# Float32r splits for the second attention products of batches 0 and 1, and for ten of sixteen first-block output products

## Chip, core and metric

The kernel runs on one core of one Trainium2 chip. The metric is the device time of one execution in microseconds, taken as the median of several runs. Engines are named as the profile names them: PE is TensorE (PEld its weight loads), DVE VectorE, ACT ScalarE, POOL GpSimd, SP SyncE, which here issues nearly all transfers.

## What is computed

The reference, cut to its core:

```python
def _attn_ref(q, k, v):            # batch 8, heads 8, seq 576, head_dim 64
    k_p = k.reshape(B, H, Sp, 8, D).mean(axis=3)      # 72 pooled rows
    v_p = v.reshape(B, H, Sp, 8, D).mean(axis=3)
    scores = scale * np.matmul(q, k_p.transpose(0, 1, 3, 2))
    attn = softmax(scores)          # exp, sum + 1e-9
    return np.matmul(attn, v_p)

x = attention output as 4608 tokens x 512
h = x @ w_in;  x = (h * cos(h)) @ w_out               # 512 -> 2048 -> 512
g = x @ w_gate; x = (silu(g) * (x @ w_val)) @ w_out2  # 512 -> 1536 -> 512
```

## The kernel before

**Stages.** The program is a start-up (attention of batch 0, conversion of the weights), then the first MLP, into which attention of batches 1 to 7 is woven, then the second MLP. The first MLP goes over 9 blocks of 512 tokens (n), each in 16 *slots* of 128 hidden columns (f). A slot (n, f) is: `pe_h` (lines 537 to 539), 12 products of 128x512 into the PSUM tile `h`; `turns` (547, 548) and `cosine` (569 to 573), which make `w` = h·cos h on ACT and DVE; `parts` (584 to 587), which splits `w` into `gh` + `gl`; and two slots later `pe_y`, which adds the slot's share of the output to the four PSUM tiles `acc`.

**Two ways of a product.** float32 data go through TensorE either as float32, one instruction that the trace shows as two MATMUL records, or as float32r, where each operand is split into a high part (an ACT cast) and a low part (a DVE subtraction) and three products are issued: high·high, high·low, low·high. `pe_y` uses float32 for `n == 0 and f < Y32` (line 599), the split else (606 to 608). `Y32` is 16 before, so all of block 0 is float32: no `parts`, no `wo_high` in it.

**Second attention product.** `do_pt` transposes the normalised probabilities `pm` of a tile of 128 (or 64) tokens into PSUM (`pt`, 64 of the 72 pooled rows of each head, and `px`, the remaining 8 rows of all heads) and copies them to `pth` and `ptx`. `prep_v` makes the stationary operands from the pooled v. `do_av` then multiplies, per pair of heads p (4 of them) and group of tokens (256 + 256 + 64 in batch 0, 256 + 320 in the others), into `av`, and ACT writes the result into `ring` (399). For batches below `ACTB` = 2, `do_av` issues two float32 products, `vmh`·`pth` and `vl1`·`ptx`; for the others five float32r products (`vmh`·`pth`, `vmh`·`ptl`, `vml`·`pth`, `vl1`·`ptx`, `vl2`·`ptx`). Batch 0's tokens, split into `xhl` (514 to 516), are the first block's input, so the first `pe_h` waits for groups 0 and 1 of batch 0.

**Order.** The first step of the program is a string of letters: `s` scores, `x` softmax, `p` transposes, `a` av products, `v` prep_v, `V0`/`K`/`U` pooled sums on DVE, `f`/`F`/`G` pieces of weight conversion (`fill`), `i`/`o` loads of weights, `X` the split into `xhl`:

```python
    "s0 s1 f4 x0 s2 p0 V0 v x1 p1 f6 s3 s4 F3 a0 x2 p2 x3 p3 a1 w i1 q G2 K0 K1 K2 U0 X i11 o2 "
    "x4 b f6 "
```

A tile scheduler then reorders the instructions on each engine by its own estimates, so that the code's order is only its input. The weights arrive as 64-bit floats in `st_i` (w_in) and `st_o` (w_out); four integer operations on ACT and DVE (477, 482, 487, 494) turn a piece of 128x512 into float32 (`ce_i`, `wo`), and for w_in lines 1010 (ACT) and 994 (DVE) split it into `wa`. The raw float32 w_out stays in `wo_raw`, from which float32 `pe_y` reads directly and `wo_high` (553) and line 586 make the split one. Batch 1's slots are 1 to 14, batch 2 begins at 17. `do_norm` (338 to 350) makes `pm`; tile 1's `pm` lies in `vst` and tiles 2 and 3's in `kst`, the buffers of raw v and k.

Of the kernel before, what the change touches and what calls it, by code (L numbers as in the profile page):

```python
# [8 lines left out]
F32 = mybir.dt.float32  # L9
F32R = mybir.dt.float32r  # L10
# [15 lines left out]
def fused_kernel(  # L26
# [18 lines left out]
    nc = tc.nc  # L45
    B, H, S, D = q.shape
# [58 lines left out]
    kT = p1a.tile([P, NP, 2 * SP], F32, name="kT")  # L105
    av_tiles = {}

    def av_tile(nm, b):

        kind = F32 if b < ACTB else F32R  # L110
        if (nm, kind) not in av_tiles:
            shape = {"v": [P, NP, P], "p": [P, NP, PTW], "x": [P, PTW]}["x" if nm == "ptx" else nm[0]]
            t = av_tiles[nm, kind] = p1a.tile(shape, kind, name=f"{nm}_{b}", tag=nm)
            if nm in ("vmh", "vml", "vl2"):
                nc.gpsimd.memset(t if kind is F32 else t.bitcast(F32), 0.0)
        return av_tiles[nm, kind]

    nc.gpsimd.memset(kT, 0.0)
    for nm in ("vmh", "vml", "vl1", "vl2", "pth", "ptl", "ptx"):
        av_tile(nm, 0)  # L120

    def raw_tile(nm):
        return chain.tile([P, 2, TB], F32, name=nm, tag="raw", bufs=2)
# [125 lines left out]
            nc.scalar.mul(to[:, :, SM:], ps[rows, 2 * P :].rearrange("d (s p) -> d p s", p=NP), -EXP_SCALE)  # L249

    def prep_v(b):
        vmh, vml, vl1, vl2 = (av_tile(nm, b) for nm in ("vmh", "vml", "vl1", "vl2"))
        vp = vps.pop(b)
        if b < ACTB:
            for r in range(2):
                rows, cols = slice(r * SM, (r + 1) * SM), slice(r * D, (r + 1) * D)
                nc.scalar.mul(vmh[rows, :, cols], vp[rows, :NP], 1.0 / POOL)
            nc.vector.tensor_mul(
                vl1[:SM].rearrange("q p (r d) -> q r p d", r=2),
                vp[:SM, NP : NP + 1].rearrange("q (a o) d -> q a o d", a=1).to_broadcast([SM, 2, NP, D]),  # L260
                mask[:SM].rearrange("q (p r o) -> q r p o", r=2, o=1).to_broadcast([SM, 2, NP, D]),
            )
            return
        for r in range(2):
            rows, cols = slice(r * SM, (r + 1) * SM), slice(r * D, (r + 1) * D)
            nc.scalar.mul(vmh[rows, :, cols], vp[rows, :NP], 1.0 / POOL)
            nc.vector.scalar_tensor_tensor(
                out=vml[rows, :, cols], in0=vp[rows, :NP], scalar=1.0 / POOL, in1=vmh[rows, :, cols],
                op0=ALU.mult, op1=ALU.subtract,
            )  # L270
        t = p1a.tile([P, H, SP], F32, name=f"vt_{b}", tag="e")[:, :, :D]
        nc.vector.tensor_mul(
            t, vp[:, NP : NP + 1].to_broadcast([P, H, D]), mask.rearrange("p (h o) -> p h o", o=1).to_broadcast([P, H, D])
        )
        t = t.rearrange("q (p r) d -> q r p d", r=2)
        h2 = vl1.rearrange("q p (r d) -> q r p d", r=2)
        l2 = vl2.rearrange("q p (r d) -> q r p d", r=2)
        for r in range(2):
            nc.scalar.copy(h2[:, r], t[:, r])
            nc.vector.tensor_sub(l2[:SM, r], t[:SM, r], h2[:SM, r])  # L280
# [49 lines left out]
    def do_norm(b, t, pm=None):  # L330
        n = TILES[t][1]
        e = es.pop((b, t))[:n]
        if b < ACTB:
            sm = sms.pop((b, t))[:n]
        else:
            sm = p1a.tile([P, H, 1], F32, name=f"sm_{b}_{t}", tag="sm", bufs=2)[:n]
            nc.vector.reduce_sum(sm[:, :, 0], e, axis=AX.X)
        nc.vector.tensor_scalar_add(sm, sm, 1e-9)
        nc.vector.reciprocal(sm, sm)
        if pm is None:  # L340
            pm = p1a.tile([P, H * SM + P], F32, name=f"pm_{b}_{t}", tag="pm")
        pms[b, t] = pm
        nc.vector.tensor_mul(
            pm[:n, : H * SM].rearrange("q (h s) -> q h s", h=H), e[:, :, :SM], sm.to_broadcast([n, H, SM])
        )

        for g in range(2):
            left = pm[:n, H * SM + g * SM : H * SM + (g + 1) * SM].rearrange("q (h s) -> q h s", h=H)
            if g == 0:
                nc.vector.tensor_mul(left, e[:, :, SM:], sm.to_broadcast([n, H, SL]))  # L350
            elif b >= ACTB:
                nc.vector.tensor_copy(pm[:n, H * SM + SM :], pm[:n, H * SM : H * SM + SM])

# [930 lines left out]
```

## Time and profile before

| | us |
|---|---|
| median of 3 runs | 1787.25 |
| runs from, to | 1786.49, 1788.84 |
| profiled execution, its own time | 1786.07 |
| its span | 1784.3 |
| PE busy in the span | 1737.2 (97%) |
| DVE busy | 1169.0 (66%) |
| ACT busy | 996.1 (56%) |

The profiled execution takes 1.8 us more than its span. In the rows below a timeline line is: start, length, engine, source line, operation, what it writes and reads, shape, count of records run together; in square brackets the idle time of the engine ahead of it and what ended that. Matmul records overlap, so the time of a product is the distance between starts. PEclk is the granted TensorE clock, 1.00 for 2.4 GHz.

### The profile page before, as it was taken

Reading aid. Unit: us, or ns where it says so; the run is one execution under the profiler, and the core shown is the slowest. Engines: PE = TensorE matmul, PEld = TensorE weight load, DVE = VectorE, ACT = ScalarE, POOL = GpSimd, SP = SyncE. Lnnn points to the kernel's source line nnn. Section 1 sums busy time; section 2 is a strip of 40 time slices with the busy share of each in tenths; the row PEclk is TensorE's granted clock in tenths of the full one; section 3 lists DMA queues with packets and bytes.
Section 4 is the critical chain, followed back from the end, with each engine's and each line's share of the span. In section 5 each row is a group of like instructions: output and inputs, shape, how many; then the busy total and the mean of one; then the engine's idle time right before and its main releaser. Section 6 shows DMA issues by size and latency. Waiting matters only on the chain.

```text
span 1784.3 us, 23241 instructions
## 1 busy us (share of the span) xinstructions
PE 1737.2 (97%) x8076; PEld 1444.5 (81%) x8076; DVE 1169.0 (66%) x2006; ACT 996.1 (56%) x1815; POOL 122.1 (7%) x217
## 2 busy tenths in 40 slices
PE   4979999999999999999999999999999999999998
PEld 3546588888888888888888778888888888999998
DVE  6695377867767677687675677853684377458346
ACT  5576477767667767677575565433443344344333
POOL 0131300403003011000000000000000000000000
PEclk9989999999999999999999999999999999999999
DMA  9553244646576455575775587675567657777772
GB/s 232 162 162 105 82 149 145 194 133 205 131 228 208 118 201 145 188 213 160 230 265 182 192 321 270 202 274 195 195 208 257 197 191 225 298 255 244 298 253 90
DMA packets 240244, 357.00 MB, mean 200 GB/s; under 512 B 141696, under 2 KB 147840, under 8 KB 240128
## 3 DMA queue, kind: packets, MB, share of 16 engines
q1 hardware_dynamic: 235440, 354.35, 61.5%
q10 hardware_dynamic: 4688, 1.18, 0.3%
q8 instruction: 64, 1.05, 0.2%
q14 instruction: 52, 0.43, 0.1%
HBM read 285.74 MB, written 69.73 MB: 199 GB/s over the span
## 4 chain that ended last, share of the span: by engine, by line
PE 89%; DMA 4%; DVE 4%; ACT 2%; issue 1%; POOL 0%; SPq 0%; ACTq 0%; DVEq 0%; POOLq 0%
PE X L791 14%; PE oX L921 8%; PE h L537 7%; PE h L538 7%; PE h L539 7%; PE acc L606 7%; PE Y L791 7%; PE acc L608 7%; PE acc L607 7%; PE oY L921 4%; PE av L393 3%; PE Z L791 3%; PE acc L599 2%; PE oZ L921 2%; PE s L308 2%; DMA w2r<-w_dram 1%
## 5 line engine op out<-in xcount | busy, mean ns | idle before, releaser
L791 PE MATMUL X<-t_P,wc 128*128 128x512 f32 (+1 forms) x1080 | 232.9, 368 | 2.3 <-ACT u L840 2.3
L537 PE MATMUL h<-xhl,wa 128*128 128x512 f32 x576 | 232.0, 403 | 1.3 <-DVE w L573 1.3
L539 PE MATMUL h<-xhl,wa 128*128 128x512 f32 x576 | 225.9, 392 | 0.0
L538 PE MATMUL h<-xhl,wa 128*128 128x512 f32 x576 | 225.9, 392 | 0.0
L791 PEld LDWEIGHTS X<-t_P,wc 128*128 128x128 f32 x1080 | 196.5, 188 | 29.1 <-ACT u L840 4.0
L606 PE MATMUL acc<-gh,wo_ring 128*128 128x512 f32 x448 | 179.3, 400 | 0.0
L607 PE MATMUL acc<-gl,wo_ring 128*128 128x512 f32 x448 | 174.8, 390 | 0.0
L608 PE MATMUL acc<-gh,wo_ring 128*128 128x512 f32 x448 | 174.8, 390 | 0.0
L547 ACT ACTIVATE w<-h,few 128x512 f32<-128x512 f32 x144 | 98.9, 687 | 121.3 <-PE h L539 121.0
L548 DVE SCALAR_TENSOR_TENSOR w<-w,h 128x512 f32<-128x512 f32 x144 | 98.2, 682 | 68.8 <-ACT w L547 68.5
L537 PEld LDWEIGHTS h<-xhl,wa 128*128 128x128 f32 x576 | 109.1, 189 | 27.8 <-issue 3.8
L573 DVE SCALAR_TENSOR_TENSOR w<-w,h 128x512 f32<-128x512 f32 x144 | 98.4, 683 | 49.9 <-ACT w L570 48.2
L538 PEld LDWEIGHTS h<-xhl,wa 128*128 128x128 f32 x576 | 108.9, 189 | 23.7 <-issue 2.4
L539 PEld LDWEIGHTS h<-xhl,wa 128*128 128x128 f32 x576 | 108.9, 189 | 23.0
L587 DVE TENSOR_TENSOR gl<-w,gh 128x512 fp32r<-128x512 f32 x128 | 90.9, 710 | 51.0 <-ACT gh L584 50.1
L584 ACT CAST gh<-w 128x512 fp32r<-128x512 f32 x128 | 78.9, 616 | 69.3 <-DVE w L573 47.3
L569 ACT ACTIVATE w<-w 128x512 f32<-128x512 f32 x144 | 91.1, 633 | 46.1 <-DVE w L548 45.1
L843 DVE TENSOR_TENSOR p<-p,X 128x512 f32<-128x512 f32 (+1 forms) x60 | 37.8, 632 | 116.8 <-PE X L791 108.6
L126 ACT CAST xhl<-pst 128x1024 fp32r<-128x1024 f32 (+1 forms) x70 | 67.7, 968 | 71.3 <-PE oX L921 26.1
L921 PE MATMUL oX<-xhl,wc 128*128 128x512 f32 (+1 forms) x480 | 102.7, 368 | 0.0
L608 PEld LDWEIGHTS acc<-gh,wo_ring 128*128 128x128 f32 x448 | 84.1, 188 | 18.6
L606 PEld LDWEIGHTS acc<-gh,wo_ring 128*128 128x128 f32 x448 | 84.2, 188 | 17.0 <-issue 0.8
(196 smaller groups left out, 3377.2 us busy)
## 6 DMA issues: line engine op xcount, KB each, us to landing
wc<-wc_dram SPq DMA_DIRECT2D x273, 512.0 KB
wo_ring<-wo_dram SPq DMA_DIRECT2D x112, 512.0 KB
wc_dram<-wc SPq DMA_DIRECT2D x42, 512.0 KB
wc_dram<-ow SPq DMA_DIRECT2D x42, 256.0 KB
y_dram<-yo SPq DMA_DIRECT2D x18, 512.0 KB
w_dram<-ce_w SPq DMA_DIRECT2D x36, 256.0 KB
st_i<-in_moe_w_in_dram SPq DMA_DIRECT2D x16, 512.0 KB
st_o<-in_moe_w_out_dram SPq DMA_DIRECT2D x16, 512.0 KB
```

The costliest lines, as they stand in the source:

```text
L537: nc.tensor.matmul(ps, whi, xhl[0][:, 0, c], start=c == 0, stop=False)
L538: nc.tensor.matmul(ps, whi, xhl[0][:, 1, c], start=False, stop=False)
L539: nc.tensor.matmul(ps, wlo, xhl[0][:, 0, c], start=False, stop=c == KC - 1)
L547: nc.scalar.activation(w, h, AF.Identity, bias=magic)
L548: nc.vector.scalar_tensor_tensor(out=w, in0=w, scalar=MAGIC, in1=h, op0=ALU.subtract, op1=ALU.subtract)
L569: nc.scalar.activation(w, w, AF.Sin, scale=PI)
L573: nc.vector.scalar_tensor_tensor(out=w, in0=w, scalar=1.0, in1=h, op0=ALU.subtract, op1=ALU.mult, reverse0=True)
L606: nc.tensor.matmul(acc[n][i], a[:, cols], xh, start=f == 0, stop=False)
L607: nc.tensor.matmul(acc[n][i], a[:, cols], xl, start=False, stop=False)
L608: nc.tensor.matmul(acc[n][i], b[:, cols], xh, start=False, stop=f == NF1 - 1)
L791: nc.tensor.matmul(ps[:, :hb], w, t[:, x, c, :hb], start=first and c == 0 and n == 0, stop=c == 1 and n == 2, skip_group_check=not first,)
L921: nc.tensor.matmul(banks[key][m][:, :hb], u, x[:, b, i, :hb], start=first_ and j == i == k == 0, stop=j == NJ - 1 and i == 1 and k == 2, s ...
```

## The change

`Y32` goes from 16 to 6: in block 0, slots 6 to 15 get `parts` (two ACT casts and two DVE subtractions a slot) and 12 float32r products in `pe_y` in place of 4 float32 ones. The branches `b < ACTB` go out of `prep_v`, `do_norm`, `do_pt`, `do_av` and `av_tile`: batches 0 and 1 get `vml`, `vl2`, `ptl`, full `ptx`, and five float32r products in place of two float32 ones. The tiles for these are made once, in float32r, and no longer again at batch 2. Lines after are 11 to 20 lower than before (537 becomes 517, 599 becomes 579).

```diff
-    Y32 = NF1
+    Y32 = 6
...
     def prep_v(b):
...
-        if b < ACTB:
-            for r in range(2):
-                rows, cols = slice(r * SM, (r + 1) * SM), slice(r * D, (r + 1) * D)
-                nc.scalar.mul(vmh[rows, :, cols], vp[rows, :NP], 1.0 / POOL)
-            nc.vector.tensor_mul(
-                vl1[:SM].rearrange("q p (r d) -> q r p d", r=2),
...
-            return
...
-            elif b >= ACTB:
+            else:
                 nc.vector.tensor_copy(pm[:n, H * SM + SM :], pm[:n, H * SM : H * SM + SM])
...
     def do_pt(b, t):
...
-        if b < ACTB:
-            nc.scalar.copy(pth[:, :, o : o + n], ps)
-            px = psum.tile([SM, n], F32, name=f"px_{b}_{t}", tag="att", bufs=2)
-            nc.tensor.transpose(px, pm[:n, NP * P : NP * P + SM], ident[:n, :n])
-            nc.scalar.copy(ptx[:SM, o : o + n], px)
-            return
         nc.scalar.copy(pth[:, :, o : o + n], ps)
         nc.vector.tensor_sub(ptl[:, :, o : o + n], ps, pth[:, :, o : o + n])
...
-        if b < ACTB:
-            terms = [(vmh, pth[:, p, o : o + n])]
-            terms += [(vl1[:SM], ptx[:SM, o : o + n])]
```

The scheduler moves instructions with this. On DVE in the start-up, from the sign step of `ce_i_3` to the normalisation of tile 1 (`vst`), the kernel before has these; `vl` is the operand for the last 8 pooled rows, `sm_1` tile 1's sums:

```order
L494 SCALAR_TENSOR_TENSOR ce_i_3_185<-st_i_3_131,ce_i_3_185 128x512
L258 TENSOR_TENSOR vl_0_97<-vp_309,few 64x2x4x64
L338 TENSOR_SCALAR sm_1_240<-sm_1_240 128x8
L487 SCALAR_TENSOR_TENSOR ce_i_0_193<-st_i_0_161,ce_i_0_193 128x512
L339 RECIPROCAL sm_1_240<-sm_1_240 128x8
L994 TENSOR_TENSOR wa_3_265<-ce_i_3_185,wa_3_265 128x512
L343 TENSOR_TENSOR vst<-vst,sm_1_240 128x512
L350 TENSOR_TENSOR vst<-vst,sm_1_240 128x64
```

After, from the first subtraction of tile 0's transposes:

```order
L352 TENSOR_TENSOR ptl<-pt_0_301,pth 128x4x128
L356 TENSOR_TENSOR ptx<-px_0_308,ptx 64x128
L256 SCALAR_TENSOR_TENSOR vml<-vp_312,vmh 64x4x64
L261 TENSOR_TENSOR vt_320<-vp_312,few 128x8x64
L974 TENSOR_TENSOR wa_3_265<-ce_i_3_185,wa_3_265 128x512
L256 SCALAR_TENSOR_TENSOR vml<-vp_312,vmh 64x4x64
L269 TENSOR_TENSOR vl_98<-vt_320,vl_97 64x4x64 x2
L327 TENSOR_SCALAR sm_1_240<-sm_1_240 128x8
L467 SCALAR_TENSOR_TENSOR ce_i_0_193<-st_i_0_161,ce_i_0_193 128x512
L328 RECIPROCAL sm_1_240<-sm_1_240 128x8
L474 SCALAR_TENSOR_TENSOR ce_i_0_193<-st_i_0_161,ce_i_0_193 128x512
L332 TENSOR_TENSOR vst<-vst,sm_1_240 128x512
```

Two subtractions on tile 0 and five more for v now stand between `ce_i_3` and tile 1's `vst`; the mask product for `vl` (258) is gone.

On PE where the first output product of block 0 stands (slot 0, `w_0`; `s_1` are batch 1's scores of tile 1, `qp` transposes of q), before:

```order
L539 MATMUL h_3_727<-xhl,wa_3_265 128x512
L308 MATMUL s_1_0_754<-kT,qT_1_656 128x144 x2
L308 MATMUL s_1_1_764<-kT,qT_1_656 128x144 x2
L599 MATMUL acc_0_696<-w_0_563,wo_449 128x512
L599 MATMUL acc_1_697<-w_0_563,wo_449 128x512
L599 MATMUL acc_2_698<-w_0_563,wo_449 128x512
L599 MATMUL acc_3_699<-w_0_563,wo_449 128x512
L293 MATMUL qp_2_774<-ident,q_453 128x128 x4
L599 MATMUL acc_0_696<-w_1_628,wo_449 128x512
```

After:

```order
L519 MATMUL h_2_727<-xhl,wa_3_265 128x512
L282 MATMUL qp_1_715<-ident,q_496 128x128 x4
L297 MATMUL s_1_0_820<-kT,qT_1_714 128x144 x2
L297 MATMUL s_1_1_830<-kT,qT_1_714 128x144 x2
L579 MATMUL acc_0_754<-w_0_607,wo_492 128x512
L579 MATMUL acc_1_755<-w_0_607,wo_492 128x512
L579 MATMUL acc_2_756<-w_0_607,wo_492 128x512
L579 MATMUL acc_3_757<-w_0_607,wo_492 128x512
L517 MATMUL h_3_793<-xhl,wa_0_139 128x512
L518 MATMUL h_3_793<-xhl,wa_0_139 128x512
```

The first output product now stands behind `h_2` and ahead of `h_3`; before it stood behind `h_3`, with slot 1's output next.

On PE, slot 6's output product (`s_3` are scores of batch 1's tile 3), before:

```order
L308 MATMUL s_3_1_1072<-kT,qT_3_902 128x144 x2
L599 MATMUL acc_0_696<-w_6_945,wo_449 128x512
L599 MATMUL acc_1_697<-w_6_945,wo_449 128x512
L599 MATMUL acc_2_698<-w_6_945,wo_449 128x512
L599 MATMUL acc_3_699<-w_6_945,wo_449 128x512
L293 MATMUL qp_4_1082<-ident,q_453 128x64 x4
```

After:

```order
L586 MATMUL acc_0_754<-gh_6_1074,wo_6_1076 128x512
L587 MATMUL acc_0_754<-gl_6_1075,wo_6_1076 128x512
L588 MATMUL acc_0_754<-gh_6_1074,wo_6_1076 128x512
L586 MATMUL acc_1_755<-gh_6_1074,wo_6_1076 128x512
L587 MATMUL acc_1_755<-gl_6_1075,wo_6_1076 128x512
L588 MATMUL acc_1_755<-gh_6_1074,wo_6_1076 128x512
L586 MATMUL acc_2_756<-gh_6_1074,wo_6_1076 128x512
L587 MATMUL acc_2_756<-gl_6_1075,wo_6_1076 128x512
L588 MATMUL acc_2_756<-gh_6_1074,wo_6_1076 128x512
L586 MATMUL acc_3_757<-gh_6_1074,wo_6_1076 128x512
L587 MATMUL acc_3_757<-gl_6_1075,wo_6_1076 128x512
L588 MATMUL acc_3_757<-gh_6_1074,wo_6_1076 128x512
```

Four float32 products on `w_6` became twelve on `gh_6` and `gl_6`.

## Rows read from the trace of the kernel before

**Rows 1.** Windows: us, busy by engine with counts, granted clock, DMA share, GB/s.

```profile
80.00:100.00 20.00, 11.58 (x54) 8.69 (x54) 19.31 (x36) 19.61 (x56) 7.22 (x9) 0.90 0.10 29
...
120.00:140.00 20.00, 15.71 (x54) 9.87 (x52) 16.34 (x28) 14.15 (x35) 7.76 (x11) 0.91 0.62 193
...
180.00:200.00 20.00, 20.00 (x65) 10.74 (x64) 4.06 (x6) 6.13 (x15) 8.47 (x17) 1.00 0.20 57
...
80.00:124.00 44.00, 33.85 (x126) 21.34 (x125) 42.23 (x74) 34.46 (x83) 18.09 (x24) 0.92 0.38 121
```

**Rows 2.** Timeline of PE, start-up to slot 6's output product (columns above).

```profile
46.55 1.19 PE L393 MATMUL av<-pth,vmh 128*128 128x256 f32 x2 [0.79 <-issue]
...
55.73 1.11 PE L361 MATMUL pt<-ident,kst 128*128 128x128 f32 x4
...
59.36 1.22 PE L393 MATMUL av<-pth,vmh 128*128 128x256 f32 x2 [0.52 <-ACT pth L363]
...
68.56 0.79 PE L537 MATMUL h<-xhl,wa 128*128 128x512 f32 x1
...
70.44 0.63 PE L538 MATMUL h<-xhl,wa 128*128 128x512 f32 x1
70.86 0.63 PE L539 MATMUL h<-xhl,wa 128*128 128x512 f32 x1
...
97.92 6.11 PE L599 MATMUL acc<-w,wo 128*128 128x512 f32 x8 [7.12 <-DVE wo L494]
...
126.55 1.03 PE L293 MATMUL qp<-ident,q 128*128 128x128 f32 x4 [4.29 <-ACT e L318]
...
149.85 2.74 PE L599 MATMUL acc<-w,wo 128*128 128x512 f32 x6
```

**Rows 3.** Timeline of PE, slot 15's float32 output, then block 1's first split one.

```profile
215.57 3.59 PE L599 MATMUL acc<-w,wo 128*128 128x512 f32 x8
219.00 1.14 PE L308 MATMUL s<-kT,qT 128*128 128x144 f32 x8
...
222.77 0.39 PE L606 MATMUL acc<-gh,wo 128*128 128x512 f32 x1
...
225.49 0.39 PE L537 MATMUL h<-xhl,wa 128*128 128x512 f32 x1
```

**Rows 4.** Timeline of PE, group 1 of batch 1, then of batch 2 (float32r).

```profile
191.20 0.70 PE L393 MATMUL av<-pth,vmh 128*128 128x320 f32 x2
...
194.03 3.70 PE L599 MATMUL acc<-w,wo 128*128 128x512 f32 x8
...
295.93 0.30 PE L393 MATMUL av<-pth,vmh 128*128 128x320 f32 x1
...
298.98 0.39 PE L537 MATMUL h<-xhl,wa 128*128 128x512 f32 x1
```

**Rows 5.** Lines on DVE: operation, tiles, count, min/median/max ns.

```profile
L369 DVE TENSOR_TENSOR ptl<-pt,pth x30: 416/683/691, 236.7 to 841.6; 128x512 fp32r<-128x512 f32 x24, 128x256 fp32r<-128x256 f32 x6
...
L373 DVE TENSOR_TENSOR ptx<-px,ptx x30: 227/294/295, 237.4 to 842.1; 64x128 fp32r<-64x128 f32 x24, 64x64 fp32r<-64x64 f32 x6
...
L267 DVE SCALAR_TENSOR_TENSOR vml<-vp,vmh x12: 408/420/423, 200.8 to 741.5; 64x256 fp32r<-64x256 f32 x12
...
L587 DVE TENSOR_TENSOR gl<-w,gh x128: 650/692/1217, 217.2 to 994.9; 128x512 fp32r<-128x512 f32 x128
```

**Rows 6.** Timeline of DVE: slot 0's turns, a slow conversion row, slot 6's last step.

```profile
75.53 0.69 DVE L548 SCALAR_TENSOR_TENSOR w<-w,h 128x512 f32<-128x512 f32 x1 [1.78 <-ACT w L547]
...
114.75 1.23 DVE L487 SCALAR_TENSOR_TENSOR wo<-st_o,wo 128x512 uint32<-128x512 uint32 x1
...
136.32 0.67 DVE L573 SCALAR_TENSOR_TENSOR w<-w,h 128x512 f32<-128x512 f32 x1
```

**Rows 7.** Timeline of POOL, the sum that ran beside the slow row.

```profile
114.63 1.66 POOL L213 TENSOR_TENSOR vraw<-vraw 128x256 f32<-128x256 f32 x2 [2.50 <-DMA vraw<-in_v_dram]
```

**Rows 8.** Waits of SP: its line, awaited engine and line, us, times, longest.

```profile
SPq L470 <- DVE v L213: 13.8, 1, 13.8
```

More of the change, by code (lines that the diff above doesn't have):

```diff
@@ L106, in fused_kernel, with av_tile @@
     av_tiles = {}
-    def av_tile(nm, b):
-        kind = F32 if b < ACTB else F32R
-        if (nm, kind) not in av_tiles:
+    def av_tile(nm):
+        if nm not in av_tiles:
             shape = {"v": [P, NP, P], "p": [P, NP, PTW], "x": [P, PTW]}["x" if nm == "ptx" else nm[0]]
-            t = av_tiles[nm, kind] = p1a.tile(shape, kind, name=f"{nm}_{b}", tag=nm)
+            t = av_tiles[nm] = p1a.tile(shape, F32R, name=nm)
             if nm in ("vmh", "vml", "vl2"):
-                nc.gpsimd.memset(t if kind is F32 else t.bitcast(F32), 0.0)
-        return av_tiles[nm, kind]
+                nc.gpsimd.memset(t.bitcast(F32), 0.0)
+        return av_tiles[nm]
     nc.gpsimd.memset(kT, 0.0)
     for nm in ("vmh", "vml", "vl1", "vl2", "pth", "ptl", "ptx"):
-        av_tile(nm, 0)
+        av_tile(nm)
     def raw_tile(nm):
@@ L251, in prep_v @@
     def prep_v(b):
-        vmh, vml, vl1, vl2 = (av_tile(nm, b) for nm in ("vmh", "vml", "vl1", "vl2"))
+        vmh, vml, vl1, vl2 = (av_tile(nm) for nm in ("vmh", "vml", "vl1", "vl2"))
         vp = vps.pop(b)
-        if b < ACTB:
-            for r in range(2):
-                rows, cols = slice(r * SM, (r + 1) * SM), slice(r * D, (r + 1) * D)
-                nc.scalar.mul(vmh[rows, :, cols], vp[rows, :NP], 1.0 / POOL)
-            nc.vector.tensor_mul(
-                vl1[:SM].rearrange("q p (r d) -> q r p d", r=2),
-                vp[:SM, NP : NP + 1].rearrange("q (a o) d -> q a o d", a=1).to_broadcast([SM, 2, NP, D]),
-                mask[:SM].rearrange("q (p r o) -> q r p o", r=2, o=1).to_broadcast([SM, 2, NP, D]),
-            )
-            return
         for r in range(2):
@@ L350, in do_norm @@
                 nc.vector.tensor_mul(left, e[:, :, SM:], sm.to_broadcast([n, H, SL]))
-            elif b >= ACTB:
+            else:
                 nc.vector.tensor_copy(pm[:n, H * SM + SM :], pm[:n, H * SM : H * SM + SM])
     def do_pt(b, t):
-        pth, ptl, ptx = av_tile("pth", b), av_tile("ptl", b), av_tile("ptx", b)
+        pth, ptl, ptx = av_tile("pth"), av_tile("ptl"), av_tile("ptx")
         t0, n = TILES[t]
@@ L376, in do_av @@
         vmh, vml, vl1, vl2, pth, ptl, ptx = (
-            av_tile(nm, b) for nm in ("vmh", "vml", "vl1", "vl2", "pth", "ptl", "ptx")
+            av_tile(nm) for nm in ("vmh", "vml", "vl1", "vl2", "pth", "ptl", "ptx")
         )
```

## Prediction

> **What bounds the kernel now.** I read the page first: PE is busy 97% of the span, so anything that takes work off PE shows, except where PE waits. Then the table of windows, to find where it waits. From 140 us on PE has no gap (180 to 200 is typical: 20.00 of 20.00, with DVE at only 4.06) [rows 1]; there a microsecond of PE work removed is a microsecond gained, and DVE and ACT have room for more. From 80 to 124 it is the other way: DVE is busy 42.23 of 44, while PE idles 8.42 us of 80 to 100 [rows 1]. Then the timeline of PE for the waits themselves: 7.12 us ahead of slot 0's output product at 97.92, for a DVE conversion step, and 4.29 us at 126.55, for ACT's exp [rows 2]. Ahead of 80 stands one chain: av of groups 0 and 1 of batch 0, the split of these tokens, the first `h` [rows 2]. So there are three stretches: a chain (to about 75), a stretch that DVE paces (to about 127), then PE alone. The change takes PE work out of all three and adds DVE and ACT work to all three. All of it must lie in the first 300 us: from about the first slots of block 1 the order on PE is the same in both kernels.
>
> **Output products, slots 6 to 15.** A float32 slot took 215.57 to 219.00, 3.43 us for 8 records; a split slot 222.77 to 225.49, 2.72 for 12 [rows 3]. Twelve cheap ones beat eight dear ones by 0.71, ten times: **-7.1**. This lies on PE's own stretch. What it adds, two DVE subtractions of 0.69 [rows 5] and two ACT casts of the same 128x512 a slot, is 1.4 on DVE in a slot in which PE has 2.7 of `h` and 2.7 of output to do; DVE, at 4.06 of 20 us there [rows 1], hides it. If that cover failed, PE would wait for `gl` in each slot and the gain would be gone. Only slot 6, the first, is at risk (below). Bounds: -7.1 and 0; I take the first, since ten equal slots later run this way.
>
> **Av products, batch 1.** Group 1 in float32: two of its four p took 191.20 to 194.03, 2.83, so 5.66 in all; the same group in float32r, batch 2's, took 295.93 to 298.98, 3.05 for 20 products [rows 4]. **-2.6**, on PE's stretch. Group 0 has 256 columns for 320, so by 0.8 an estimated 4.5 against 2.4: **-2.1**.
>
> **Av products, batch 0.** Group 0 lasted 46.55 to 55.73 and group 1 59.36 to 68.56, 9.2 each for 16 records, 0.57 a record [rows 2]. Its clock is the question. The windows print 1.00 there, but the `h` products right behind, at 70.44 and 70.86, lie 0.42 apart [rows 2] where one costs 0.227 (2.72/12) later [rows 3]; so this stretch runs at the lower level, 1.2 GHz. At it a float32r product of 256 columns costs half of 0.42, and 20 take 4.2; at the upper level 3.05 x 0.8 = 2.4. I take 4.2: -5.0 per group, -10.0 before what the change puts in the way. That is on DVE. Ahead of tile 1's `pm`, which `pt_1` and so group 0 need, now stand `ptl` 0.68, `ptx` 0.29, two `vml` of 0.42 [rows 5] and two subtractions for `vl2` of the same size as those (0.84 by it); `vt` takes the place of the mask product for `vl` and is taken as even. Sum 2.65: group 0 starts about 49.2 and ends 53.4, 2.3 earlier. For tiles 2 and 3 the two PSUM buffers are held until `ptl` and `ptx` are done, about 1.0 more (0.68 + 0.29): group 1 starts about 58.1 and ends 62.3 in place of 68.56. **Net -6.3**, between -3.5 (each of the two delays costs 1.4 more, half as much again, as the chain passes between DVE, ACT and PE) and -9.9 (both groups at the upper level, 1.8 each). Group 2 of 64 columns has no row of its size; it lies in a stretch where PE waits anyway, 0, bounds +1 and -1.
>
> **The stretch that DVE paces.** What happens to PE's waits there, 8.42 + 4.29 us, decides the rest. The new order puts slot 0's output product, 3.43 us of work [rows 3], ahead of `h_3`, into what was the 7.12 us wait; I count it as filling that: **-3.4**, bounds 0 and -7. Against this stands the added DVE work. Between slot 0's turn (75.53) and slot 6's last step (136.32, 0.67 long) [rows 6] the order adds tile 4's two subtractions (0.42 + 0.23, the smallest of their rows), those of two tiles of batch 1 (2 x 0.97), the v split (1.7), small copies of `pm` (0.2 each by their size against the rows, four), and slot 6's own `gl` and `wo` (1.4); two `wo` subtractions of block 1 that stood there are moved out (-1.4). Net about +5. So `gl_6` is ready at 137.0 - 6.3 + 5 = 135.7, plus the cast ahead of it, at most another 0.7: 136.4. PE by its own terms gets to slot 6's output at 149.85 [rows 2] - 6.3 - 2.1 - 3.4 = 138.0. The two are close, with 1.6 us to spare: the forecast stands, but DVE is next in line.
>
> A conversion step that took 0.68 elsewhere took 1.23 at 114.75, while POOL ran a pooling sum from 114.63 [rows 6, 7]. The Trainium skill (SBUF — State Buffer, "Who interferes with whom") says that a DVE instruction with two SBUF inputs contends with a GpSimd instruction that reads SBUF, and that one with at most one SBUF input does not. The trace agrees: the row that waited reads its two inputs from SBUF. Of what is added in this stretch, `ptl` and `ptx` read PSUM and one SBUF tile and would by it go free; `vml`, `vl2` and slot 6's two subtractions read two SBUF tiles, and at 0.55 each (1.23 - 0.68) would take some 3 us more, past the spare 1.6, which would move the sum by about +1.5.
>
> **Loads.** SP waits 13.8 us for a v sum on DVE ahead of a weight load [rows 8], and that sum stands behind the added start-up work: about 3 to 5 later. These weights are for later slots; hidden as long as DVE is behind with its conversions. This is the price of a rival.
>
> **Sum.** -7.1 - 2.6 - 2.1 - 6.3 - 3.4 = -21.5. Against the profiled execution's own 1786.07 that is 1764.6; the median of the runs shown is 1.2 higher, so 1764.5 to 1766. I write 1765.
>
> **Rivals.**
> R1, *the early gain is eaten*: DVE, saturated, gets 5 more us of work, its conversions start no earlier because the loads come 3 to 5 later, and slot 6's output starts at 149.85 as before. Then only -7.1 - 2.6 is left: 1776.4. For it: 42.23 of 44 [rows 1], the spare 1.6; against: the 4.29 us wait at 126.55 is for ACT, not DVE, and DVE has gaps ahead of 80 (1.78 at 75.53 [rows 6]).
> R2, *the clock rises earlier*: batch 0's float32r stretch brings the upper level, so that group 1 costs 2.4 (-1.8), the first six `h` products 0.2 less each (-1.2), and the whole 7.12 wait is filled (-3.7 more): 1758. For it the Trainium skill (TensorE: Matmul & The Clock Gate, Part 1) says that the throttled state is the default and activity releases it. The trace so far is against: dense float32 from 46 to 68 did not raise it [rows 2].
> R3, *slower*: the late v sum delays the weight loads by 5.2, DVE work grows by 5, contention adds 3.2, all in series, and slot 6's output starts at 149.85 + 13.4 = 163.3. With -9.7 behind it the time is 1789.8. It decides from a start of about 163 on; the spare of DVE ahead of 80 speaks against all three adding up.
> R4, *it does nothing*: PE waits for `gl` in each split slot, or the float32r products cost as much as the float32 ones; 1784 to 1788. Rows 3 and 4 speak against both.
>
> **How the numbers follow.** A measurement of this kernel can tell about 0.2%, 3.6 us, from no change. Forecast 0.55 (1760 to 1770), R1 0.26 (1771 to 1780), R2 0.11 (1753 to 1760), R3 0.04, R4 0.04. The forecast's own terms at their bounds reach 1758 and 1771; the range takes in most of R1 and half of R2: 1755 to 1778. Faster: 0.92; same 0.04 (R4); slower 0.04 (R3).
>
> **What would show it.** After: slot 0's `h` some 6 us earlier than 68.56; the batch 0 groups at 4 to 5 us each (2.4: R2); slot 0's output at 85 to 93, with its wait under 4 us; slot 6's output at 136 to 140 (at 149 or later R1, past 163 R3); from there on PE without gaps, and 2.7 for a slot's output. I would be wrong if PE's idle time in 75 to 130 grew, with DVE named as what ended it.

## The result, and the profile after

| | before | after |
|---|---|---|
| median, us | 1786.95 of 4 runs | 1766.3 of 4 runs (1765.3 to 1766.96) |
| ratio after / before, 95% interval | | 0.9882 (0.9865 to 0.9899) |
| profiled execution, its span | 1786.07, 1784.3 | 1766.96, 1765.2 |

20.65 us less by the medians, 19.1 between the two profiled executions (the profiled one after is the longest of its four). The first line of the page of the changed kernel, busy time by engine:

```profile
PE 1716.2 (97%) x8136; PEld 1453.4 (82%) x8136; DVE 1194.8 (68%) x2064; ACT 1008.6 (57%) x1839; POOL 126.6 (7%) x214
```

PE's busy time fell by 21.0, from 1737.2 to 1716.2, and its idle time grew by 1.9 (the span is 19.1 shorter), so the gain is PE work taken out; DVE grew from 1169.0 to 1194.8 and ACT from 996.1 to 1008.6. The windows of the changed kernel (us, busy by engine with counts, granted clock, DMA share, GB/s):

```profile
80.00:124.00 44.00, 37.53 (x131) 23.77 (x130) 39.99 (x72) 33.32 (x88) 24.98 (x33) 0.88 0.43 139
100.00:130.00 30.00, 23.62 (x83) 15.08 (x82) 25.83 (x49) 22.42 (x61) 15.20 (x23) 0.89 0.49 152
104.00:113.00 9.00, 5.74 (x17) 4.74 (x18) 6.79 (x13) 6.18 (x14) 4.28 (x6) 0.62 0.53 158
140.00:220.00 80.00, 79.97 (x378) 64.94 (x377) 62.54 (x116) 64.87 (x140) 21.46 (x33) 1.00 0.41 120
```

In 80 to 124 PE is now busy 37.53 (33.85 before) and DVE 39.99 (42.23 before, [rows 1]). In 140 to 220 PE still has no gap, though DVE is now busy 62.54 of 80. A new thing stands between: in 104 to 113 PE is busy 5.74 of 9 at a granted clock of 0.62. PE's idle time in 75 to 130, whose growth was to be the sign of a wrong forecast, fell from 13.1 to 9.4. The timeline of PE, for the rows that answer to [rows 2], and at the end group 1 of batch 1 and a split output (compare [rows 3, 4]):

```profile
50.10 0.55 PE L373 MATMUL av<-pth,vmh 128*128 128x256 f32 x1 [0.78 <-issue]
50.45 0.41 PE L373 MATMUL av<-ptl,vmh 128*128 128x256 f32 x1
50.66 0.41 PE L373 MATMUL av<-pth,vml 128*128 128x256 f32 x1
...
58.95 0.58 PE L373 MATMUL av<-pth,vmh 128*128 128x256 f32 x1 [1.53 <-DVE ptl L352]
...
62.31 0.63 PE L517 MATMUL h<-xhl,wa 128*128 128x512 f32 x1
...
63.81 0.63 PE L517 MATMUL h<-xhl,wa 128*128 128x512 f32 x1
...
65.01 0.40 PE L517 MATMUL h<-xhl,wa 128*128 128x512 f32 x1
...
67.08 0.38 PE L241 MATMUL kps<-ident,kp 128*128 128x128 f32 x2
...
85.93 5.11 PE L579 MATMUL acc<-w,wo 128*128 128x512 f32 x8 [1.52 <-DVE wo L474]
...
107.26 1.11 PE L350 MATMUL pt<-ident,pm 128*128 128x128 f32 x4 [3.41 <-ACT e L307]
...
108.23 0.78 PE L517 MATMUL h<-xhl,wa 128*128 128x512 f32 x1
108.81 0.63 PE L518 MATMUL h<-xhl,wa 128*128 128x512 f32 x1
109.23 0.63 PE L519 MATMUL h<-xhl,wa 128*128 128x512 f32 x1
...
113.14 1.02 PE L579 MATMUL acc<-w,wo 128*128 128x512 f32 x2
...
127.87 0.50 PE L517 MATMUL h<-xhl,wa 128*128 128x512 f32 x1 [2.96 <-DVE w L553]
...
140.19 0.50 PE L586 MATMUL acc<-gh,wo 128*128 128x512 f32 x1
...
178.44 0.30 PE L373 MATMUL av<-pth,vmh 128*128 128x320 f32 x1
...
179.90 0.39 PE L586 MATMUL acc<-gh,wo 128*128 128x512 f32 x1
```

Group 0 starts at 50.10 (46.55 before) and lasts 4.5, to 54.61 (9.2 before); its products lie 0.21 apart, the lower level. (The windows print a granted clock of 1.00 for 50 to 55 and 0.51 for 60 to 65, with the same spacing in both, so the level is read from the spacing.) Group 1 starts at 58.95 (59.36) and the first `h` product at 62.31 (68.56). That one stands ahead of group 1's last p, and the other `h` products follow from 63.81 on. A mark that stands in the same place in both orders is the first `kps`, the transposes behind slot 0's `h`: 67.08 here, and before

```profile
73.26 0.38 PE L242 MATMUL kps<-ident,kp 128*128 128x128 f32 x2
```

The first output product comes at 85.93 (97.92), 12.0 earlier. Then 3.41 us of waiting for ACT's exp at 107.26, an `h` behind it whose products lie 0.43 apart (108.23 to 113.14, 4.9 us), and 2.96 us of waiting for DVE at 127.87. Slot 6's output starts at 140.19, where it was 149.85: 9.66 of 12.0 are left. Behind that two p of group 1 take 1.46 (178.44 to 179.90, 2.83 before) and a split output 2.75, 179.90 to 182.65 (3.43 before). On DVE, one of the new rows twice, two older ones and slot 6's last step:

```profile
94.28 0.41 DVE L269 TENSOR_TENSOR vl<-vt,vl 64x256 fp32r<-64x256 f32 x1
...
95.55 0.95 DVE L269 TENSOR_TENSOR vl<-vt,vl 64x256 fp32r<-64x256 f32 x1
...
106.63 0.79 DVE L462 TENSOR_SCALAR wo<-wo 128x512 uint32<-128x512 uint32 x1 [1.19 <-ACT wo L457]
...
109.00 0.67 DVE L528 SCALAR_TENSOR_TENSOR w<-w,h 128x512 f32<-128x512 f32 x1
...
134.07 0.69 DVE L567 TENSOR_TENSOR gl<-w,gh 128x512 fp32r<-128x512 f32 x1
```

and on POOL, the sums beside all but the last:

```profile
94.32 3.09 POOL L212 TENSOR_TENSOR kraw<-kraw 128x256 f32<-128x256 f32 x2 [1.45 <-DMA kraw<-in_k_dram]
...
106.41 1.32 POOL L212 TENSOR_TENSOR vraw<-vraw 128x256 f32<-128x256 f32 x2 [3.33 <-DMA vraw<-in_v_dram]
...
108.49 2.11 POOL L212 TENSOR_TENSOR vraw<-vraw 128x256 f32<-128x256 f32 x2
```

`gl_6` was ready at 134.8, 5.4 before PE came to it. The `vl2` subtraction, 0.41 by its median, took 0.95 beside a POOL sum and 0.41 beside the same sum's start. The integer step at 106.63, which reads one SBUF tile, took 0.79 (0.42 where POOL was idle). The step at 109.00, which reads PSUM and one SBUF tile, kept its usual time beside a sum.

### The profile page after: what moved, and what is told of

Read it like the earlier page. It is cut to its first block, busy times and chain, and to the rows that moved or that the text cites. A ratio compares the mean times of both kernels' runs of the same rounds, so it can differ in the third digit from the quotient of the medians.

```text
span 1765.2 us, 23440 instructions
## 1 busy us (share of the span) xinstructions
PE 1716.2 (97%) x8136; PEld 1453.4 (82%) x8136; DVE 1194.8 (68%) x2064; ACT 1008.6 (57%) x1839; POOL 126.6 (7%) x214
## 4 chain that ended last, share of the span: by engine, by line
PE 90%; DVE 4%; DMA 3%; ACT 2%; issue 1%; ACTq 0%; SPq 0%; DVEq 0%
PE X L771 15%; PE oX L901 8%; PE h L517 7%; PE acc L586 7%; PE Y L771 7%; PE h L518 7%; PE h L519 7%; PE acc L588 7%; PE acc L587 7%; PE oY L901 4%; PE Z L771 4%; PE av L373 3%; PE s L297 3%; PE oZ L901 2%; DMA w2r<-w_dram 1%; PE pt L350 1%
## 5 line engine op out<-in xcount | busy, mean ns | idle before, releaser
L567 DVE TENSOR_TENSOR gl<-w,gh 128x512 fp32r<-128x512 f32 x138 | 97.7, 708 | 51.1 <-ACT gh L564 50.2
L564 ACT CAST gh<-w 128x512 fp32r<-128x512 f32 x138 | 85.1, 617 | 71.5 <-DVE w L553 51.5
```

Of the source, the lines that this page charges most:

```text
L567: nc.vector.tensor_sub(b, w, a)
```

## What the experiments asked

The theory on trial, A: the parts of the sum add; what lies behind slot 6 is PE work and fixed; what lies ahead is a chain (to the first `h`) and a stretch that DVE paces. The rivals: the y part did it by its order (B), its splits are not hidden (C), batch 0 doesn't matter (D), ACT's exp holds group 0 (E), and for the new wait at 107.26: it holds back ready work (F), or is only one face of DVE's pace (G), or has another end close behind (K), or comes from the queue of loads on SP (J); and, for the whole stretch, ACT's exp and PE's own order set its pace and not DVE (H). Two marks are read from every timeline: the start of slot 6's output, and what is left of the span from there.

| kernel | median, us | of before beside it | ratio, 95% interval | slot 6's output starts | span from there |
|---|---|---|---|---|---|
| before | | | | 149.85 | 1634.4 |
| changed | 1766.3 | 1786.95 | 0.9882 (0.9865, 0.9899) | 140.19 | 1625.0 |
| e1 av alone | 1773.08 | 1785.94 | 0.9920 (0.9905, 0.9935) | 139.60 | 1631.6 |
| e2 y alone | 1778.59 | 1785.94 | 0.9957 (0.9942, 0.9971) | 151.38 | 1626.7 |
| e3 batch 1's av alone | 1782.04 | 1785.94 | 0.9978 (0.9969, 0.9988) | 147.93 | 1633.0 |
| e4 Y32 = 0 | 1769.80 | 1785.94 | 0.9908 (0.9894, 0.9923) | 143.31 | 1626.9 |
| e5 v split later | 1767.38 | 1785.77 | 0.9898 (0.9882, 0.9915) | 139.92 | 1625.7 |
| e6 splits doubled | 1766.92 | 1785.77 | 0.9898 (0.9883, 0.9913) | 140.27 | 1625.7 |
| e7 pt_0 behind h_5 | 1761.51 | 1785.77 | 0.9865 (0.9850, 0.9880) | 137.74 | 1623.9 |
| e8 tile 4's scores late | 1765.36 | 1785.77 | 0.9891 (0.9876, 0.9905) | 138.42 | 1625.5 |
| e9 e7 and e8 | 1760.34 | 1785.72 | 0.9856 (0.9841, 0.9871) | 133.59 | 1625.2 |
| e10 less on DVE | 1762.30 | 1785.72 | 0.9867 (0.9851, 0.9884) | 131.53 | 1626.9 |
| e11 e9 and e5 | 1767.90 | 1785.72 | 0.9900 (0.9883, 0.9916) | 140.11 | 1625.3 |
| e12 raw loads on POOL | 1765.66 | 1785.63 | 0.9887 (0.9870, 0.9903) | 139.67 | 1625.0 |

The last two columns are of one profiled execution each. With both parts the last one is 1624 to 1627 whatever is done ahead of slot 6; apart from these 3 us the differences lie in the column before it.

### One part alone (e1, e2, e3)

```diff
--- e1, against the changed kernel
-    Y32 = 6
+    Y32 = NF1
--- e2, against the kernel before
-    Y32 = NF1
+    Y32 = 6
--- e3, against the kernel before
+    AVB = 1
-        if b < ACTB:
+        if b < AVB:
```

In e3 `AVB` stands for `ACTB` in `av_tile`, `prep_v`, `do_pt`, `do_av` and the copy in `do_norm`.

> The changed kernel with all 16 output products of block 0 in float32 again (Y32 = 16): the av part alone. Theory A (the parts add, as the sum had them): slot 6's output at 140 as in the changed kernel (9.7 us earlier than before), 2.6 for batch 1's group 1 behind it: 12.3 faster than before, about 1774.7. Rival B (the y part brought the early gain by its other order of instructions): under 8 faster, above 1779.

> The kernel before with Y32 = 6 alone: the y part alone. Theory A: ten slots at 0.71, 7.1 faster, about 1779.9, slot 6's output where it was (149.9) and its twelve products 2.7 to 2.9 long. Rival B: 10 or more faster. Rival C (the added subtractions and casts are not hidden): 4 or less.

> The kernel before with float32r av products for batch 1 alone (batch 0 stays float32, its operands are made again in float32r at batch 1). Theory A: group 1's 2.6 for certain, group 0's 2.1 if DVE's added work up to slot 6 doesn't eat it: 2.6 to 4.7 faster, 1782.3 to 1784.4; so that batch 0's part of the early gain is the difference to the av-only kernel, 8 to 10. Rival D (batch 0's shorter products don't reach the end, batch 1's do it all): 10 or more faster.

Measured by the medians: -12.9, -7.4 and -3.9, against 12.3, 7.1 and 2.6 to 4.7. The parts add: 12.9 + 7.4 = 20.3 beside 20.65 for the whole, and by difference batch 0 is worth 12.9 - 3.9 = 9.0. Where they lie is as the sum had it: e1 brings slot 6 10.3 earlier and saves only 2.8 behind it (batch 1's group 1, 2.6), e2 takes 7.7 off what is behind and brings slot 6 no earlier (151.38). A's sums hold; B, C and D fall.

### The first six outputs split too (e4)

```diff
-    Y32 = 6
+    Y32 = 0
```

> The changed kernel with Y32 = 0: the first six output products split as well. By PE's work alone 6 x 0.71 less, 4.3 faster than the changed kernel, about 1762. Theory A (DVE is next in line up to slot 6): 1.4 more DVE work in each of six slots of a stretch that it paces, 8 us, less 4.3: not faster than the changed kernel, 1766 to 1771, with PE's idle time between 75 and 140 up by 4 or more.

1769.8: 3.5 above the changed kernel (16.1 below its own kernel before, against 20.65), with 4.3 us less PE work. Slot 6's output starts 3.1 later, and PE's idle time in 75 to 140 is 12.8 for 9.4, a little less than the 4 more that A asked for. PE's longest wait from 60 us on (line, awaited engine and line, us, times, longest):

```profile
PE acc L587 <- DVE gl L567: 7.0, 4, 3.6
```

and the window in which it lies (columns as above):

```profile
100.00:130.00 30.00, 20.71 (x87) 15.07 (x86) 29.91 (x50) 21.17 (x54) 20.29 (x25) 0.94 0.41 134
```

DVE is busy 29.91 of 30 and PE only 20.71 (25.83 and 23.62 in the changed kernel); PE waits for `gl`, 7.0 us, where the changed kernel has no such wait. In this stretch a split that saves PE 0.71 costs more than it saves. That is why it matters which slots get it.

### The splits of slots 6 to 15 done twice (e6)

```diff
         nc.vector.tensor_sub(b, w, a)
+        if not n:
+            nc.vector.tensor_sub(wo[s][:, 1], wo_raw[f // 8][:, f % 8], wo[s][:, 0])
+            nc.vector.tensor_sub(b, w, a)
```

> The changed kernel with the two subtractions of each slot 6 to 15 done twice: 1.4 us more on DVE in a slot, 13.7 in all, nothing else. Theory A (DVE hides the split of these slots): no more than 2 slower than the changed kernel, 1766 to 1768. Rival C (it is the next bound there too): 5 to 14 slower, 1771 to 1780, with PE waiting for gl.

1766.92, unchanged: 20 more subtractions, 13.7 us of work on DVE, cost nothing that shows. The window of those slots (columns as above):

```profile
140.00:220.00 80.00, 78.66 (x372) 63.61 (x371) 70.50 (x128) 61.41 (x134) 21.91 (x33) 1.00 0.42 122
```

DVE is at 70.50 of 80 and PE, at 78.66, has lost 1.3 at most. So the added subtractions of the change are hidden there, with as much again to spare; C falls for good.

### What holds group 0 (e5, e8)

```diff
--- e5
-        "s0 s1 f4 x0 s2 p0 V0 v x1 p1 f6 s3 s4 F3 a0 x2 p2 x3 p3 a1 w i1 q G2 K0 K1 K2 U0 X i11 o2 "
+        "s0 s1 f4 x0 s2 p0 V0 x1 p1 v f6 s3 s4 F3 a0 x2 p2 x3 p3 a1 w i1 q G2 K0 K1 K2 U0 X i11 o2 "
--- e8
-        "s0 s1 f4 x0 s2 p0 V0 v x1 p1 f6 s3 s4 F3 a0 x2 p2 x3 p3 a1 w i1 q G2 K0 K1 K2 U0 X i11 o2 "
+        "s0 s1 f4 x0 s2 p0 V0 v x1 p1 f6 s3 F3 a0 x2 p2 x3 p3 a1 s4 w i1 q G2 K0 K1 K2 U0 X i11 o2 "
```

> The changed kernel with the v split of batch 0 written behind tile 1's normalisation and transposes in the start-up string: two of the seven added DVE rows (vt, 0.60, and the two vl, 0.75) and one conversion row come behind tile 1's pm instead of ahead of it. Theory A (what stands ahead of tile 1's pm on DVE is what holds group 0 back): pt_1 some 2.5 us earlier than 40.1, group 0 from 50.1 to about 47.6, the first h as much earlier, 1.5 to 2.5 faster than the changed kernel: 1764 to 1765. Rival E (ACT's exp of tile 3, for which the scores of tile 4 wait, holds group 0): group 0 within 0.5 of 50.1, time unchanged.

> The changed kernel with the scores of batch 0's tile 4 written behind group 1 instead of ahead of group 0: on PE group 0 follows tile 3's scores at once. Theory E (those scores wait for ACT's exp and hold group 0 back): group 0 starts at about 45.5 for 50.1, the first h 2 to 4.5 earlier; the time 1 to 4 less than the changed kernel's, 1762 to 1765, the rest lost where DVE paces. Rival A (DVE's rows ahead of tile 1's pm hold it): group 0 earlier than 48 all the same, but group 1 no earlier, since the pm of tiles 2 and 3 come when they came: time unchanged within 1.

The timeline of PE in e5:

```profile
38.11 1.09 PE L350 MATMUL pt<-ident,vst 128*128 128x128 f32 x4 [3.83 <-DVE vst L339]
...
44.82 1.22 PE L297 MATMUL s<-kT,qT 128*64 128x144 f32 x4 [1.68 <-ACT kst L307]
...
50.35 0.55 PE L373 MATMUL av<-pth,vmh 128*128 128x256 f32 x1 [2.58 <-issue]
...
59.91 0.28 PE L373 MATMUL av<-pth,vmh 128*128 128x256 f32 x1
...
60.54 0.38 PE L373 MATMUL av<-pth,vmh 128*128 128x256 f32 x1
```

and of ACT, the first exp of tile 4:

```profile
48.95 0.32 ACT L307 ACTIVATE e<-s,mx 64x72 f32<-64x72 f32 x1 [2.45 <-DVE sm L327]
```

Tile 1's transposes come at 38.11, 2.0 earlier than in the changed kernel, and tile 4's scores too (44.82 for 46.88). Yet group 0 starts at 50.35, as in the changed kernel. Tile 4's exp waits until 48.95 for DVE's work on the sums `sm`, which by the code have two buffers, so that tile 4's needs tile 2's; and the PSUM bank that group 0 writes is, by the code, the one that this exp reads. The profile names no releaser for group 0, only "issue", but the fourth exp of that tile (the last to read the bank) ends 0.1 ahead of it in both runs, first the changed kernel, then e5:

```profile
49.80 0.20 ACT L307 ACTIVATION_READ_ACCUMULATOR e<-s,mx 64x1 f32 x1
...
50.05 0.20 ACT L307 ACTIVATION_READ_ACCUMULATOR e<-s,mx 64x1 f32 x1
```

E's mark came, though not by E's path: the scores of tile 4, which it had waiting for tile 3's exp, came 2 us earlier too. A's mark did not come: the DVE rows ahead of tile 1's `pm`, my 2.65, do delay tile 1's transposes, but with some of them gone another wait, tile 4's exp, ended as late. In e8, with those scores out of the way:

```profile
47.27 0.55 PE L373 MATMUL av<-pth,vmh 128*128 128x256 f32 x1 [1.73 <-ACT kst L307]
...
55.75 0.39 PE L373 MATMUL av<-pth,vmh 128*128 128x256 f32 x1 [1.53 <-DVE ptl L352]
```

Group 0 starts at 47.27, group 1 at 55.75, both some 3 us earlier, slot 6's output 1.8 earlier; the time, 1765.36, can't be told from the changed kernel's and just misses E's 1762 to 1765, while A's mark, group 1 no earlier, was missed by 3 us. Here too group 0 follows the exp that reads its bank by 0.1 (tile 3's fourth, which ended at 47.17).

e5 also shows what the rival on the clock was worth. In e5 two p of group 1 lie 0.63 apart (59.91, 60.54), the upper level, where they lay 1.07 apart in the changed kernel (60.18, 61.25), and the last p starts at 61.54 for 62.74. Behind it PE waited 0.71 for DVE's split of the tokens, and slot 6's output came at 139.92 for 140.19: that level, so early, left nothing that shows at slot 6.

### The new wait at 107.26 (e7, e9, e11)

```diff
+    mids[4].remove((run_item, (1, ("pt", 0))))
+    norms[4].remove((run_item, (1, ("norm", 1))))
+    mids[5][:0] = [(run_item, (1, ("pt", 0))), (run_item, (1, ("norm", 1)))]
```

This stands behind the tables of slots, ahead of `run_slot`.

> The changed kernel with the transposes of batch 1's tile 0 (and the normalisation of tile 1) one slot later, so that on PE h_5 stands ahead of pt_0. In the changed kernel PE waits 3.41 us at pt_0 for ACT's exp, and runs h_5 behind it at the lower clock level, 4.9 for 2.8. Theory F (that wait holds back work that is ready, and costs the clock too): 2 to 5 faster, 1761 to 1764. Rival G (DVE paces this stretch, so PE waits somewhere else): unchanged within 1, with the wait at the next h or output product.

1761.51, 4.8 below the changed kernel by the medians, within F (its runs are 1759.3 to 1763.3, the profiled one 3.6 below the changed kernel's). The timeline of PE in e7 (`h_5` at 103.84, `pt_0` at 107.00):

```profile
103.84 0.80 PE L521 MATMUL h<-xhl,wa 128*128 128x512 f32 x1
...
107.00 0.60 PE L350 MATMUL pt<-ident,pm 128*128 128x128 f32 x4
```

and its longest wait from 60 us on:

```profile
PE h L521 <- DVE w L557: 4.6, 1, 4.6
```

The wait at `pt_0` is gone and `h_5` takes 3.2 us, where it took 4.9 behind the wait. G is right in part: a wait of 4.6 for DVE has opened one `h` later. Slot 6's output starts 2.4 earlier.

> The changed kernel with both reorderings: batch 0's tile 4 scores behind group 1, batch 1's tile 0 transposes behind h_5. One took 24 off the kernel before, the other 20, against 21 for the changed kernel. Theory F (each takes out a wait of its own): 1 to 2 below the better one, 1759.5 to 1760.5, with slot 6's output at about 136. Rival G (DVE's rows up to slot 6 end where they end): as the better one alone, 1761 to 1762, and slot 6's output at 137.5 or later.

1760.34 (1759.88 to 1762.76): the fastest here, 0.9856 of before, and its runs don't overlap those of the changed kernel (1765.3 to 1766.96). PE in e9:

```profile
111.38 0.50 PE L521 MATMUL h<-xhl,wa 128*128 128x512 f32 x1 [4.42 <-DVE w L557]
```

It still waits 4.42 for DVE at `h`, but slot 6's output starts at 133.59, 6.6 earlier than in the changed kernel, where G had 137.5 or later; by that mark F. By the time F and G can't be told apart: beside e7 alone the gain is 1.2 by the medians, within the intervals.

> The kernel of both reorderings and in addition batch 0's v split behind tile 1's normalisation. Theory E (with tile 4's scores out of the way, tile 1's pm holds group 0 after all): group 0 starts at about 45.2, 2 us earlier than the 47.3 that it had with tile 4's scores alone moved, and the time is 0 to 1.5 below that of both reorderings. Rival A2 (another wait, ACT's exp of tile 3, holds it): group 0 at 47 or later, time unchanged within 1.

This failed: 1767.9, 7.6 above e9. The first product of group 0 did start earlier (44.48, which speaks for E and against A2), but the scheduler, with other estimates, put `h_3` ahead of slot 0's output again and moved the first `h` products. PE's longest wait in e11 from 40 us on:

```profile
PE h L522 <- DVE xhl L500: 4.5, 1, 4.5
```

A wait of 4.5 for the split of the tokens, where e9 has 1.7; slot 0's output begins at 87.20 for 82.43 in e9. So its time can't say what an earlier group 0 would be worth in e9; it says that an edit of the order's input moves more than what it names.

### Less DVE work (e10)

```diff
             nc.scalar.mul(vmh[rows, :, cols], vp[rows, :NP], 1.0 / POOL)
+            if b == 1:
+                continue
...
+            if b != 1:
                 nc.vector.tensor_sub(l2[:SM, r], t[:SM, r], h2[:SM, r])
...
+        if b != 1:
             nc.vector.tensor_sub(ptl[:, :, o : o + n], ps, pth[:, :, o : o + n])
```

> The changed kernel without some of the new DVE rows of batch 1: vml (2 rows), vl2 (2 rows) and ptl (one row a tile) are left out, so that its products read batch 0's values there (a part of the computation left out); the products on PE are all there. 2.6 us less on DVE up to slot 6's output (4 x 0.34 and 2 x 0.60). Theory A (DVE paces 85 to 140): slot 6's output 2 to 3 earlier than 140.2 and the time as much lower, 1763.5 to 1764.5. Rival H (ACT's exp and PE's own order pace it): slot 6's output within 1 of 140.2, the time unchanged within 1.

1762.3, 4.0 below the changed kernel. The window 80 to 124 of e10:

```profile
80.00:124.00 44.00, 39.07 (x153) 24.67 (x152) 43.80 (x78) 37.75 (x89) 27.93 (x37) 1.00 0.50 162
```

H's mark did not come: with 2.6 us less on DVE ahead of it slot 6's output comes 8.7 earlier. But this is far more than A's 2 to 3, and DVE, with less to do, is busier in the window (43.80 of 44, 39.99 in the changed kernel), so it had gaps there that closed. The order changed with the edit (slot 2's output now stands behind `pt_0`), as in e9, where the order alone brought 6.6, and the clock of the window is 1.00 for 0.88. How the 8.7 divides was not measured; the run does not tell A from H. The profiled execution, the fastest of its four, keeps 6.8 of it (the span from slot 6 on is 1.9 longer), the medians 4.0.

### The loads (e12)

In the changed kernel ACT has a wait just ahead of the exp for which PE waits:

```profile
105.94 0.66 ACT L457 ACTIVATE wo<-st_o 128x512 f32<-128x512 f32 x1 [3.10 <-DMA st_o<-in_moe_w_out_dram]
```

and on SP the load that it waits for, issued at 101.21, stands behind one of batch 2's raw loads:

```profile
100.55 0.52 SPq L186 DMA_DIRECT2D vraw<-in_v_dram  x1
101.21 0.49 SPq L450 DMA_DIRECT2D st_o<-in_moe_w_out_dram  x1
```

```diff
+        queue = nc.gpsimd if b == 2 else nc.sync
...
-                nc.sync.dma_start(t[x * SM : (x + 1) * SM], kview[b][i // 2, x, :, i % 2])
+                queue.dma_start(t[x * SM : (x + 1) * SM], kview[b][i // 2, x, :, i % 2])
...
```

> The changed kernel with batch 2's raw k and v loads issued by POOL (whose sums they wait for) in place of SP. In the changed kernel the load of a w_out piece is issued at 101.2, behind two of these loads that wait for POOL, though its buffer is free at 98.3; it lands at 105.9, ACT waits 3.10 for it with the exp of batch 1's tile 1 queued behind, PE waits 3.41 for that exp, and h_5 runs behind this at the lower level. Theory J (the queue on SP is where the 3.41 comes from): that load goes out near 98.4, ACT's wait is under 1, slot 6's output starts at 135 to 138 for 140.2, and the time is 2 to 5 below the changed kernel's, 1761.5 to 1764. Rival K (PE's wait has another end close behind, DVE's or ACT's own work): the load is earlier, slot 6's output within 1 of 140.2, the time unchanged within 1.

1765.66 and slot 6's output at 139.67: unchanged, as K had it. But J was not put to the test: the load still went out late. In e12 SP has nothing but weight loads to issue there, and waits for DVE to free their buffers; the load in question:

```profile
100.86 0.33 SPq L451 DMA_DIRECT2D st_o<-in_moe_w_out_dram  x1
```

On DVE's timeline, a slow row and the one that frees the buffer of that load:

```profile
92.99 1.65 DVE L975 TENSOR_TENSOR wa<-wo,wa 128x512 fp32r<-128x512 f32 x1
...
100.12 0.67 DVE L475 SCALAR_TENSOR_TENSOR wo<-st_o,wo 128x512 uint32<-128x512 uint32 x1
```

And PE's wait for the exp:

```profile
107.61 1.12 PE L283 MATMUL qp<-ident,q 128*128 128x128 f32 x4 [5.11 <-ACT e L308]
```

DVE was 2.5 us later with the conversion (100.12 for 97.62), so the load went out at 100.86 in place of 98.4, right behind it, and PE waited 5.11. Why DVE was later is not shown: the slow row is part of it, but in this profiled execution group 0 already started 1.9 later (51.99). What part SP's order has in the 3.41 of the changed kernel stays open.

## Why the prediction was right, step by step

**Output products**, -7.1: e2 measured 7.4 and its place. The cover by DVE, which I costed at nothing, is shown by e6. I had read its room from 180 to 200, the emptiest stretch (4.06 of 20); over 140 to 220 DVE was busy 35.72 of 80 before, which still left enough.

**Batch 1's av**, -2.6 and -2.1: the split product behind slot 6 took 1.46 for 2.83 a half, 2.7 in all, and e1's rest behind slot 6 is 2.8. Both groups together are 3.9 in e3, against 4.7.

**Batch 0's av**, net -6.3: the first `h` product started 62.31 for 68.56, 6.25 earlier, and the `kps` behind slot 0's `h` 67.08 for 73.26, 6.2 earlier. The size was right by some luck, for two errors cancel in it. The products themselves were done only 5.2 earlier: group 1 ended at 63.81 with one `h` product of 0.43 inside it, 63.38 for 68.56. Group 0's later start was 3.55 for my 2.65, and the groups lasted 4.5 and 4.4 for 4.2. The missing 1.0 came from a term that I had put only into R2: slot 0's `h` ran at the upper level from 65.01 on (nine products in 2.07, 0.23 each), where before its products still lay 0.42 apart at 70.86. I put the later start of group 0 on DVE's rows ahead of tile 1's `pm`; e5 took two of the larger ones away and group 0 stayed, because tile 4's exp, by then waiting for DVE's sums, ended no earlier. The level of the groups was as read from the spacing, 0.21 a product.

**The stretch that DVE paces**, -3.4: this is the term that was mis-sized. Slot 0's output did fill the old wait (85.93 for 97.92, 12.0 earlier, in the range that I gave for it), but of this only 9.66 was left at slot 6 (140.19, at the edge of the 136 to 140 that I gave), where the sum had 11.8; over the 6.2 of batch 0 and 2.0 of batch 1's group 0 that makes -1.5 for the term. What stands against it in the trace is a wait that I didn't name, 3.41 at 107.26 for ACT's exp, with the lower clock behind it (4.9 for the 3.2 of e7), and 2.96 at 127.87; behind slot 0's output the kernel before had one such wait, the 4.29 at 126.55. I had read the old wait at 126.55 as ACT's and used it only as an argument against R1; the same kind of wait came back 19 us earlier. Between the two profiled executions 9.66 ahead of slot 6 and 9.4 behind it stand against 11.8 and 9.7 in the sum, so nearly all of the miss is this term; its bounds, 0 and -7, held it. By the medians it was 20.65 against 21.5.

**Who was next in line.** I gave `gl_6` 136.4 and PE 138.0; it was 134.8 and 140.19. DVE's chain to slot 6 was not what ended last there. That DVE alone paces the stretch is not shown. More work on it costs (e4, 3.5), but in 100 to 130 it is busy only 25.83 of 30, and the order on PE brought slot 6 2.4 and 6.6 earlier with no DVE row less (e7, e9). Waits for DVE and for ACT's exp hold PE by turns, and which of them sets the end was not separated.

**Contention.** The rule of the Trainium skill (SBUF — State Buffer, "Who interferes with whom"), that a DVE instruction with two SBUF inputs contends with a GpSimd read, fits the 0.95 for 0.41, but not each such row waits: the same subtraction kept its 0.41 at 94.28, and of eight conversion steps `wo<-st_o,wo` that POOL's work covered for nine tenths or more (60 to 300 us) three took 0.81 to 1.22 and five 0.67 to 0.68. Its other half I had quoted too widely: the section frees an instruction with at most one SBUF input only outside the 2-port modes, which it says copies and `tensor_scalar` can enter. The trace agrees in so far as the integer step with one SBUF input took 0.79 for 0.42 beside a sum, while the seven steps `w<-w,h` that read PSUM kept 0.67 to 0.69; which mode a row ran in is not shown. So 0.55 for each added row was too simple a price, and the +1.5 can't be told apart in the time.

**Loads.** SP's wait for the v sum is as long as before:

```profile
SPq L450 <- DVE v L212: 13.5, 1, 13.5
```

13.5 for 13.8; the later sum did not become the bound as R3 wanted. R1 (nothing left of the early gain) fell: 9.66 of it is left. R2: groups 0 and 1 stayed at the lower level, as the trace of before had it, and only slot 0's `h` rose; where group 1 did run at the upper one (e5, e8) the end didn't move by what it saved. R4 fell with e2 and e3.

## What to carry to other kernels

Make the sum for each stretch by what ends last in it, and carry a mark (here the start of slot 6's output) through every run: what lies behind the mark is worth its full price, what lies ahead only what is left of it there. A split that trades PE work for DVE work pays where PE has no gaps and costs where PE waits for DVE; the same edit gained 0.7 a slot from slot 6 on (e2) and lost 0.6 a slot ahead of it (e4). Where work is ready behind a wait on an in-order engine, putting it in front was worth 4.8 (e7), as much as the change of batch 1's products (3.9, e3). When a sum of terms comes out right, look for a mark that stands in the same place in both orders: here two errors of 1 us cancelled in one term.

## What was not expected of the hardware

After PE's 3.41 us wait the granted clock fell to 0.62 over 104 to 113, and the 12 products of `h_5` took 4.9 us, where the same ones took 3.2 in e7 with no such wait: a wait of 3.4 cost 5.1. I could have read this ahead, for behind the 4.29 us wait at 126.55 the kernel before shows the same (columns as above, the granted clock 0.59):

```profile
126.00:130.00 4.00, 3.45 (x11) 2.87 (x12) 2.82 (x5) 3.97 (x15) 2.82 (x5) 0.59 0.55 179
```

In e12, where POOL also issued transfers, a DVE row of the `wa` split took 1.65 at 92.99, for 0.69 where POOL was idle; POOL was issuing two loads at 92.28 and then summing; which of the two it met is not shown.
